# Token mix of batches 2 to 7: the last products of two chunks in the array's row halves, and beta1's term added to x by GpSimd

## The chip, the cores and the metric

The kernel runs on one core of one Trainium2 chip. The metric is the device time of one execution in microseconds (us), as a median of several. All of the work is written out by hand: every instruction stands in one engine's queue in the order in which the program emits it, and the engines wait for one another by semaphores. The engines are TensorE (PE; its weight loads are PEld), VectorE (DVE), ScalarE (ACT), GpSimd (POOL) and SyncE (SP), whose only task here is to issue transfers.

## What is computed

Attention over pooled keys and values, and then a token-mixing and a channel-mixing layer:

```python
B, H, S, D = 8, 8, 576, 64        # d_model = 512
k_p, v_p = mean of k, v over groups of 8 tokens          # 72 each
x = softmax(q @ k_p.T / 8) @ v_p, heads side by side     # (8, 576, 512)
a1 = alpha1 * x + beta1
tok = einsum('ts,bsd->btd', w_tok, a1)
u = x + lam * tok
a2 = alpha2 * u + beta2
out = u + lam * (relu(a2 @ w_ch1) @ w_ch2)               # w_ch1 512x2048
```

A batch has 576 tokens: 4 chunks of 128 and a rest of 64. In the mix, `lam * tok` is a product of `w_tok` with `lam * alpha1 * x`, plus a term of beta1 alone: the sum of the row t of `w_tok`, times `lam * beta1`.

## The kernel before, in words

**Chunks and blocks.** Batches go in pairs. A pair has nine chunks of 128 tokens: four of the even batch, four of the odd one, and a mixed one made of the 64 last tokens of both (c = 4). The 36 chunks are cut into NBLK = 9 blocks of four. The loop at the end of the program goes over the blocks: block n does the channel mix (`mlp_A`, `mlp_B`) of its 512 tokens, and beside it the attention and the token mix of batch b = n + 1, which later blocks need. Blocks 7 and 8 have no attention beside them.

**Order.** In each block everything is put in a list `todo` of pairs (due time, function), and the list is sorted by due time and called in that order. This is the order in which all engines get their instructions. `mlp_A(n, j)` is due at j, for j from 0 to 15, with four products of 128x512 into a PSUM bank; the 16 parts of `mlp_B` are due at 16 to 31, four products each. `attention(b)` (a function in the program) gives the due times of the rest: `sum_k` and `att_K` (keys), `att_V` (values), `att_S4` (the scores of four heads, in row halves of the array) with its exponentials `exp(k)` on ScalarE, `att_AV` (a head's output, into `x`), `att_X` and `rest_X` (`xs`, which is `x * lam * alpha1` in bf16), `mix_T` (a chunk's token mix), `mix_uT` (the transpose of its result, for `mlp_A`), `cast_rem` and `att_Frem` (the last 64 tokens of q and k of the next batch: cast on POOL, and their q transposed by a transfer).

**The token mix.** `mix_T(b, c)` adds up five products into one bank `ps_tok`. Four take 128 tokens each. The fifth takes the 64 last tokens. For an even batch these lie in rows 0 to 63 of `xs[:, 4]`, row 64 holds `lam * beta1`, and row 64 of `wtT[:, 4]` holds the row sums of `w_tok`: 65 rows give the product and beta1's term together. For an odd batch the tokens lie in rows 64 to 127 with the beta1 row at row 0 (`wtT[:, 5]`), and all 128 rows are used. In the mixed chunk the two batches' halves of the output go to columns 0 to 63 and 64 to 127 of the array, side by side, ten products in all. VectorE then adds `x` (`u_sb`, L613) and multiplies by alpha2 (`u_bf`, L616); SP issues the transpose of `u_bf` (L625, into `u_fm`).

**Queues.** SP's queue carries, in due order, the outputs (L695, L699), the u_fm transposes (L625), the rem_qT transpose (L415), the transposes of the next batch's q (qT, L391), and the loads of v (L160), of k (L93) and of the remainders (L148). An issue in it that waits holds up all behind it. POOL's queue carries the loads of q (L79), `sum_k` (L183, L185), some of `att_X` (L577, L570) and `cast_rem` (L168, L171).

**Buffers.** `x_tm` has one buffer for a pair of batches, six sections of 128 tokens; an even batch uses sections 1 to 5, an odd one 0 to 4. `u_sb` has twelve buffers, q_bf four. All banks of PSUM but two come from one pool of six (`gp`).

Of the kernel before, what the change touches and what calls it, by code (L numbers as in the profile page):

```python
# [7 lines left out]
FP = mybir.dt.float32  # L8
F16 = mybir.dt.float16
BF = mybir.dt.bfloat16  # L10
AF = mybir.ActivationFunctionType
ALU = mybir.AluOpType
AX = mybir.AxisListType

P = 128
SPG = 72
DM = 512
# [6 lines left out]
def kernel(  # L24
# [18 lines left out]
    nc = tc.nc  # L43
    ctx.enter_context(tc.manual_schedule())
    B, H, S, D = q.shape

    const = ctx.enter_context(tc.tile_pool(name="const", bufs=1))
# [4 lines left out]
    def gp(name):  # L52
        return psA.tile([P, 512], FP, tag="gp", name=name)
# [11 lines left out]
    st1 = {}  # L65
# [307 lines left out]
    def setup_bias(js):  # L373
        ps_bias = gp("ps_bias")
        for i, jc in enumerate(js):
            for cc in range(4):
                nc.tensor.matmul(out=ps_bias[0:P, i:i + 1], lhsT=w1_of(cc, jc),
                                 rhs=b2c_bf[:, cc:cc + 1], start=(cc == 0), stop=(cc == 3))
        nc.scalar.copy(out=bias_cols[:, js[0]:js[-1] + 1], in_=ps_bias[0:P, 0:len(js)])
# [120 lines left out]
    def att_S4(b, u):  # L500

        st = st1[b]
        qT, kp, rest = st["qT"][u], kp_pool[u], st["rem_qT"]
        lo = [psB.tile([P, DM], FP, tag="ch", bufs=2, name="ps_s") for _ in range(2)]
        hi = [gp("ps_s") for _ in range(2)]
        r = [gp("ps_r")[0:SPG, 0:128].rearrange("p (h i) -> p h i", i=64) for _ in range(2)]

        def main(i):
            for a in range(2):
                rows = slice(64 * a, 64 * a + 64)  # L510
                nc.tensor.matmul(  # L511
                    out=(hi if i > 1 else lo)[a][0:SPG, 256 * (i % 2):256 * (i % 2) + 256],
                    lhsT=kp[rows, i, :], rhs=qT[rows, 2 * i:2 * i + 2, :])

        def rests(i):
            for a in range(2):
                rows = slice(64 * a, 64 * a + 64)
                nc.tensor.matmul(  # L518
                    out=r[a][:, i // 2], lhsT=kp[rows, i + a, :],
                    rhs=rest[rows, :, 2 * u + i // 2::4].rearrange("p c i -> p i c"))  # L520

        pairs = ((lo, 0), (hi, 2)) if u else ((hi, 2), (lo, 0))
        main(pairs[0][1])
        rests(pairs[0][1])
        main(pairs[0][1] + 1)
        main(pairs[1][1])
        rests(pairs[1][1])
        main(pairs[1][1] + 1)
        ET = ET_pool[u]
        for i in range(4):  # L530
            st["ET"][4 * u + i] = ET[:, i]

        def exp(k):
            if k < 2:
                o, i = ET[:, k::2, 512:S], r[k]
            else:
                a, (pair, h) = k % 2, pairs[k // 2 - 1]
                o = ET[:, h:h + 2, 256 * a:256 * a + 256]
                i = pair[a][0:SPG, :].rearrange("p (h i) -> p h i", i=256)
            nc.scalar.activation(out=o, in_=i, func=AF.Exp, bias=0.0, scale=0.125)  # L540

        st["exp", u] = exp

    def att_AV(b, h):
        st = st1[b]
        if "x" not in st:
            st["x"] = st1[b - 1]["x"] if b % 2 else work.tile([P, 6, DM], FP, tag="x_tm", bufs=1, name="x_tm")
        hp, hh = h // 2, h % 2
        ET, vp1, x = st["ET"][h], vp1_pool[hp], st["x"]
        ps_av = gp("ps_av")  # L550
        av = ps_av[:, 0:5 * 66].rearrange("p (c x) -> p c x", x=66)
        odd = b % 2
        for c in range(4):
            m0 = 256 * (c % 2) + 128 * (c // 2)
            nc.tensor.matmul(out=av[:, odd + c, :], lhsT=ET[:, m0:m0 + 128],  # L555
                             rhs=vp1[:, hh, :])

        r0 = 512 - 64 * odd
        nc.tensor.matmul(out=av[:, 4 - 4 * odd, :], lhsT=ET[:, r0:r0 + 128], rhs=vp1[:, hh, :])  # L559
        rec = work.tile([P, 5], FP, tag="rec", bufs=2, name="rec")  # L560
        nc.vector.reciprocal(out=rec, in_=av[:, :, 64:65])  # L561
        dd = D * h
        nc.vector.tensor_tensor(out=x[:, 1 - odd:6 - odd, dd:dd + D], in0=av[:, :, 0:64],  # L563
                                in1=rec.unsqueeze(2).to_broadcast((P, 5, D)), op=ALU.mult)

    def rest_X(b, h0, h1, eng=nc.vector):

        x, xs = st1[b]["x"], xs_pool[b % 2]
        cols, p0 = slice(D * h0, D * h1), 64 * (b % 2)
        eng.tensor_tensor(out=xs[p0:p0 + 64, 4, cols], in0=x[p0:p0 + 64, 5 - 5 * (b % 2), cols],  # L570
                          in1=lamal_bc[p0:p0 + 64, cols], op=ALU.mult)

    def att_X(b, h0, h1, eng=nc.vector, rest=True):

        x, xs = st1[b]["x"], xs_pool[b % 2]
        cols = slice(D * h0, D * h1)
        eng.tensor_tensor(  # L577
            out=xs[:, 0:4, cols], in0=x[:, 1:5, cols],
            in1=lamal_bc[:, cols].unsqueeze(1).to_broadcast((P, 4, D * (h1 - h0))), op=ALU.mult)
        if rest:  # L580
            rest_X(b, h0, h1, eng)


    st2 = {}
# [11 lines left out]
    def keep_warm(count):  # L596

        ps = psB.tile([P, DM], FP, tag="ch", bufs=2, name="ps_warm")
        for _ in range(count):
            nc.tensor.matmul(out=ps, lhsT=warm[:, 0:P], rhs=warm)  # L600

    def mix_T(b, c, eng=nc.vector):
        key, s = chunk_of(b, c)
        ps_tok = gp("ps_tok")
        parts = ((b % 2, 0, P),) if c < 4 else ((0, 0, 64), (1, 64, P))
        for sc in range(5):
            for i, p0, p1 in parts:
                kk, at = (P, sc) if sc < 4 else (P, 5) if i else (65, 4)
                nc.tensor.matmul(out=ps_tok[p0:p1], lhsT=wtT[0:kk, at, P * c:P * c + p1 - p0],  # L609
                                 rhs=xs_pool[i][0:kk, sc, :], start=(sc == 0), stop=(sc == 4))  # L610
        for i, p0, p1 in parts:
            x = st1[b - b % 2 + i if c == 4 else b]["x"]
            nc.vector.tensor_tensor(out=s["u"][p0:p1, :],  # L613
                                    in0=x[p0:p1, 1 + c if c < 4 else 5 - 5 * i, :],
                                    in1=ps_tok[p0:p1, 0:DM], op=ALU.add)
        eng.tensor_tensor(out=s["u_bf"], in0=s["u"], in1=al2_bc, op=ALU.mult)  # L616
# [172 lines left out]
    def attention(b):  # L789
# [11 lines left out]
        if b < B - 1:  # L801
            at = 28.5 if first else 10.0
            todo.append((at, lambda: att_F(b + 1, 0)))
            todo.append((at + 0.1, lambda: att_F(b + 1, 2)))
            todo.append((25.6 if first else 24.5, lambda: cast_rem(b + 1, nc.gpsimd)))
            todo.append((27.5, lambda: att_Frem(b + 1)))
        for u in range(2):
            todo.append((3.6 + 0.1 * u if first else -0.9 + 1.2 * u,
                         lambda u=u: sum_k(b, u, nc.gpsimd)))
# [2 lines left out]
        for u in range(2):  # L812
            at = (9.0 if first else 6.3, 13.6)[u]
            todo.append((at, lambda u=u: att_S4(b, u)))
            for k, dt in enumerate((0.1, 0.1, 0.1, 0.7, 1.7, 1.75) if u else (0.1, 0.1, 0.1, 1.1, 2.1, 3.1)):
                todo.append((at + dt, lambda u=u, k=k: st1[b]["exp", u](k)))
            early = (5.7, 6.2, 4.2, 4.7) if first else (5.7, 6.2, 2.9, 3.4)
            for i, dt in enumerate((2.9, 3.4, 4.6, 5.1) if u else early):
                h = 4 * u + i
                todo.append((at + dt, lambda h=h: att_AV(b, h)))  # L820
                if i % 2:
                    eng = nc.gpsimd if h == 5 or first and h < 5 else nc.vector
                    todo.append((at + dt + 0.1, lambda h=h, eng=eng: att_X(b, h - 1, h + 1, eng)))
        if first:
            for i, u in enumerate((0, 2, 1)):
                todo.append((10.6 + 0.1 * i, lambda u=u: sum_v(b, u)))
            for u in range(2):
                todo.append((12.3 + 1.0 * u, lambda u=u: first_V(b, u)))
        for hp in range(0 if first else 4):
            todo.append((0.2 + 2.0 * hp, lambda hp=hp: att_V(b, hp)))  # L830
        for c in range(5):
            at = 21.0 + 1.3 * c
            if c < 4 or b % 2:
                todo.append((at, lambda c=c: mix_T(b, c)))
                key = (b, c) if c < 4 else (b - 1, 4)
                todo.append((at + 1.8, lambda key=key: mix_uT(key)))
        return todo

    for n in range(NBLK):
# [11 lines left out]
        if n == 0:  # L851
            todo.append((6.2, lambda: setup_rowsum(4)))
            todo.append((8.3, setup_wtok_odd))
            for g in range(2, 4):
                todo.append((4 * g - 0.8, lambda g=g: setup_bias(range(4 * g, 4 * g + 4))))
        if n == NBLK - 1:
            for g in range(4):
                todo.append((2.0 + 3.0 * g, lambda g=g: scale_w2(g)))
# [48 lines left out]
```

## Time and profile before

| what | us |
|---|---|
| median of 3 runs (345.4 to 347.31) | 345.45 |
| the profiled execution | 346.01 |
| its span | 344.3 |
| block 0 with the end of the start-up, 27.7 to 67.8 | 40.1 |
| block 1, mix of batch 2 | 35.4 |
| block 2, mix of batch 3 and the mixed chunk | 36.8 |
| block 3, mix of batch 4 | 35.4 |
| block 7, channel mix alone | 27.6 |

The page comes from one profiled execution, which is 0.56 us above the median. Blocks are read off the chain of work in order of time, at the first `ps_h` of each. A row of the timeline gives a start, a length, an engine and what it does; a row of the list of waits gives who waited for whom, the sum, how often, and the longest. The clock granted to TensorE is 1.0 through the whole span.

### The profile page before, as it was taken

To read this page: it belongs to the slowest core of one execution; us is meant where nothing else is said; L and a number is where in the kernel's file an instruction comes from. 1 tells how busy PE (TensorE), PEld (TensorE's weight loads), DVE (VectorE), ACT (ScalarE), POOL (GpSimd) and SP (SyncE) were. 2 spreads that over 40 slices of the span, in tenths; PEclk is the share of its full clock that TensorE was granted. 3 is DMA by queue.
4 is the path that set the end of the run, shared out by engine and by line. 5 is a ranking of instruction groups with operands and counts; after the bars stand their busy time and mean duration, and the time that the engine had idled before them with its cause. 6 is when DMAs were issued, how large, how long until landed. Compare 5 with 4: busy or idle time off the path is not lost.

```text
span 344.3 us, 5882 instructions
## 1 busy us (share of the span) xinstructions
PE 336.2 (98%) x2204; PEld 177.4 (52%) x2204; DVE 221.2 (64%) x477; ACT 146.8 (43%) x277; POOL 94.8 (28%) x110
## 2 busy tenths in 40 slices
PE   7999999999999999999999999899999999999995
PEld 2768754455445544455455544454455445545544
DVE  6772478975868586866776688558675882037511
ACT  3767950089007910484038402680089006604700
POOL 8869367310162014501260217002600100000000
PEclk9999999999999999999999999999999999999999
DMA  8999979959589816794789257971900132011012
GB/s 119 198 211 275 275 142 276 172 138 161 147 233 178 148 30 184 154 208 48 208 171 179 48 170 153 190 110 61 252 32 1 47 76 76 2 61 62 2 52 70
DMA packets 66030, 45.76 MB, mean 133 GB/s; under 512 B 34345, under 2 KB 56237, under 8 KB 66002
## 3 DMA queue, kind: packets, MB, share of 16 engines
q1 hardware_dynamic: 51716, 32.73, 40.3%
q0 software_dynamic: 13824, 12.40, 22.2%
q8 instruction: 17, 0.28, 0.3%
q10 hardware_dynamic: 462, 0.27, 0.3%
q14 instruction: 11, 0.09, 0.1%
HBM read 38.30 MB, written 9.44 MB: 139 GB/s over the span
## 4 chain that ended last, share of the span: by engine, by line
PE 86%; DMA 7%; DVE 4%; issue 1%; POOL 0%; ACT 0%; SPq 0%; DVEq 0%; POOLq 0%
PE ps_h L651 35%; PE ps_ch L686 29%; PE ps_tok L609 10%; DMA u_fm<-u_bf 3%; PE ps_av L555 2%; PE ps_s L511 2%; DMA rem_qT<-rem_q 2%; DMA q_bf<-in_q_dram 2%; DVE u_sb L613 1%; PE ps_ch L675 1%; DVE u_bf L616 1%; PE ps_kp L439 1%; PE ps_r L518 1%; PE ps_sc L491 1%; DVE ps_ch L692 1%
## 5 line engine op out<-in xcount | busy, mean ns | idle before, releaser
L657 ACT ACTIVATE Hj<-ps_h,bias_cols 128x512 bf16<-128x512 f32 x144 | 98.2, 688 | 165.5 <-PE ps_h L651 163.9
L651 PE MATMUL ps_h<-u_fm,w 128*128 128x512 bf16 (+2 forms) x608 | 133.6, 368 | 0.7 <-DMA u_fm<-u_bf 0.3
L686 PE MATMUL ps_ch<-w,Hj 128*128 128x512 bf16 x560 | 130.9, 379 | 0.0
L651 PEld LDWEIGHTS <-w 128*128 128x128 bf16 x608 | 65.5, 114 | 52.0 <-issue 4.1
L686 PEld LDWEIGHTS <-Hj 128*128 128x128 bf16 x560 | 52.9, 98 | 61.7 <-issue 1.6
L609 PE MATMUL ps_tok<-xs,wtT 128*128 128x512 bf16 (+3 forms) x200 | 44.9, 380 | 0.1
L577 POOL TENSOR_TENSOR xs<-x_tm,lamal_bc 128x512 bf16<-128x512 f32 x12 | 15.2, 1269 | 107.9 <-DVE x_tm L563 107.8
L692 DVE TENSOR_TENSOR ps_ch<-lam_bc,ps_ch 128x512 f32<-128x512 f32 x32 | 22.1, 692 | 32.4 <-PE ps_ch L686 32.2
L613 DVE TENSOR_TENSOR u_sb<-x_tm,ps_tok 128x512 f32<-128x512 f32 (+1 forms) x40 | 27.3, 683 | 11.2 <-PE ps_tok L609 11.2
L561 DVE RECIPROCAL rec<-ps_av 128x5 f32<-128x5 f32 x64 | 12.3, 192 | 34.4 <-PE ps_av L559 34.1
L563 DVE TENSOR_TENSOR x_tm<-ps_av,rec 128x320 f32<-128x320 f32 x64 | 31.5, 491 | 2.7
L693 DVE TENSOR_TENSOR u_sb<-u_sb,ps_ch 128x512 f32<-128x512 f32 x35 | 24.0, 687 | 13.6 <-PE ps_ch L686 12.5
L540 ACT ACTIVATE ET<-ps_s 72x512 f16<-72x512 f32 x56 | 32.3, 592 | 0.0
L616 DVE TENSOR_TENSOR u_bf<-u_sb,al_bc 128x512 bf16<-128x512 f32 x34 | 26.2, 770 | 3.2 <-DMA u_fm<-u_bf 2.1
L609 PEld LDWEIGHTS <-wtT 128*128 128x128 bf16 (+3 forms) x200 | 17.3, 100 | 21.2 <-issue 1.7
L479 DVE TENSOR_TENSOR v_u<-v_u 72x512 f32<-72x512 f32 (+1 forms) x48 | 26.4, 550 | 0.8
L183 POOL TENSOR_TENSOR k_raw<-k_raw 128x512 f32<-128x512 f32 x14 | 18.2, 1303 | 10.0 <-DMA k_raw<-in_k_dram 10.0
L185 POOL TENSOR_TENSOR k_bf<-k_raw 128x512 bf16<-128x512 f32 x14 | 18.8, 1343 | 1.1
L555 PEld LDWEIGHTS <-ET 72*128 72x128 f16 x256 | 13.9, 97 | 9.3 <-DVE vp L472 0.6
L79 POOL DMA_DIRECT2D q_bf<-in_q_dram x16 | 12.6, 792 | 14.2 <-DVE v_u L158 13.4
L555 PE MATMUL ps_av<-vp,ET 72*128 72x66 f16 x256 | 15.6, 193 | 0.0
L577 DVE TENSOR_TENSOR xs<-x_tm,lamal_bc 128x512 bf16<-128x512 f32 x20 | 14.8, 738 | 0.7
(130 smaller groups left out, 215.8 us busy)
## 6 DMA issues: line engine op xcount, KB each, us to landing
out_dram<-u_sb SPq DMA_DIRECT2D x32, 256.0 KB
k_raw<-in_k_dram SPq DMA_DIRECT2D x12, 512.0 KB
v_u<-in_v_dram SPq DMA_DIRECT2D x12, 512.0 KB
q_bf<-in_q_dram POOLq DMA_DIRECT2D x16, 256.0 KB, 6.2
w<-in_moe_w_ch_dram POOLq DMA_DIRECT2D x6, 512.0 KB, 12.7
w<-in_moe_w_ch_dram POOLq DMA_DIRECT2D x1, 1024.0 KB, 14.5
k_raw<-in_k_dram POOLq DMA_DIRECT2D x2, 512.0 KB, 16.8
v_main<-in_v_dram POOLq DMA_DIRECT2D x1, 1024.0 KB, 11.6
```

Of the source, the lines that this page charges most:

```text
L479: nc.vector.tensor_tensor(out=t[:, :, 0:n], in0=t[:, :, 0:n], in1=t[:, :, n:2 * n], op=ALU.add)
L540: nc.scalar.activation(out=o, in_=i, func=AF.Exp, bias=0.0, scale=0.125)
L555: nc.tensor.matmul(out=av[:, odd + c, :], lhsT=ET[:, m0:m0 + 128], rhs=vp1[:, hh, :])
L563: nc.vector.tensor_tensor(out=x[:, 1 - odd:6 - odd, dd:dd + D], in0=av[:, :, 0:64], in1=rec.unsqueeze(2).to_broadcast((P, 5, D)), op=ALU.mult)
L577: eng.tensor_tensor(out=xs[:, 0:4, cols], in0=x[:, 1:5, cols], in1=lamal_bc[:, cols].unsqueeze(1).to_broadcast((P, 4, D * (h1 - h0))), op= ...
L609: nc.tensor.matmul(out=ps_tok[p0:p1], lhsT=wtT[0:kk, at, P * c:P * c + p1 - p0], rhs=xs_pool[i][0:kk, sc, :], start=(sc == 0), stop=(sc == 4))
L613: nc.vector.tensor_tensor(out=s["u"][p0:p1, :], in0=x[p0:p1, 1 + c if c < 4 else 5 - 5 * i, :], in1=ps_tok[p0:p1, 0:DM], op=ALU.add)
L616: eng.tensor_tensor(out=s["u_bf"], in0=s["u"], in1=al2_bc, op=ALU.mult)
L651: nc.tensor.matmul(out=ps_h[:, t0:t1 + one], lhsT=w1_of(cc, j), rhs=rhs, start=(cc == 0), stop=(cc == 3))
L657: nc.scalar.activation(out=t, in_=ps_h, func=AF.Relu, bias=bias_cols[:, j:j + 1], scale=1.0)
L686: nc.tensor.matmul(out=ps, lhsT=Hj[n, j][:, 128 * m:128 * m + 128], rhs=w2[j // 4][:, j % 4, :], start=(j == 0), stop=(j == NJ - 1))
L692: nc.vector.tensor_tensor(out=ps, in0=lam_bc, in1=ps, op=ALU.mult)
```

## The change

The 64 last tokens of batches 2 to 7 are now written to both halves of the rows: `exp` writes their scores twice, `att_AV` gives all 128 rows of the fifth section, and `rest_X` writes 128 rows of `xs`. In `mix_T`, chunks go in pairs (0 and 1, 2 and 3). With the even chunk go its four full products, and then both chunks' fifth products, one from rows 0 to 63 (`wtT[0:64, 4]`), one from rows 64 to 127 (`wtT[64:128, 5]`), into two banks; with the odd chunk go its four full products alone. In the mixed chunk the fifth products take 64 rows each.

The term of beta1 leaves the product. `load_be1` loads beta1 on SP at 28.2 of block 0, into a buffer of `u_sb`. At 1.6 and 2.0 of block 1, POOL multiplies it by lam, TensorE turns the row sums into columns by six products (`setup_rcol`), ScalarE copies them, and POOL makes `tokc`, six sections of 128x512. In each of blocks 1 to 6, POOL adds `tokc` to `x` in place: heads 0 to 3 in one instruction at 12.7, after their `xs` are made; heads 4 to 7 in five instructions from 18.9.

Three due times move: the mix of batch 1 from 21.0 + 1.3c to 20.8 + 1.2c (with its transposes 1.8 later each), and `att_Frem` from 27.5 to 26.22 in block 0 and 26.72 in the others.

```diff
         def exp(k):
             if k < 2:
                 o, i = ET[:, k::2, 512:S], r[k]
+                if b > 1:
+                    o = ET[:, k::2, 512:S + 64].rearrange("p h (r i) -> p h r i", i=64)
+                    i = i.unsqueeze(2).to_broadcast((SPG, 2, 2, 64))
...
-        r0 = 512 - 64 * odd
+        r0 = 512 if b > 1 else 512 - 64 * odd
...
-        eng.tensor_tensor(out=xs[p0:p0 + 64, 4, cols], in0=x[p0:p0 + 64, 5 - 5 * (b % 2), cols],
-                          in1=lamal_bc[p0:p0 + 64, cols], op=ALU.mult)
+        rows = slice(p0, p0 + 64) if b < 2 else slice(0, P)
+        eng.tensor_tensor(out=xs[rows, 4, cols], in0=x[rows, 5 - 5 * (b % 2), cols],
+                          in1=lamal_bc[rows, cols], op=ALU.mult)
...
+    def load_be1():
+        late["be1"] = work.tile([P, DM], FP, tag="u_sb", bufs=12, name="be1_bc")
+        late["tokc"] = const.tile([P, 6, DM], BF, tag="wt_bf", name="tokc")
+        nc.sync.dma_start(out=late["be1"], in_=moe_beta1.unsqueeze(0).to_broadcast((P, DM)))
+
+    def setup_rcol():
+        nc.gpsimd.tensor_tensor(out=late["be1"], in0=late["be1"], in1=lam_bc, op=ALU.mult)
+        ps = gp("ps_rc")
+        for i, t0 in enumerate((448, 0, 128, 256, 384, 512)):
+            nc.tensor.matmul(out=ps[:, i:i + 1], lhsT=wtT[64:65, 4, t0:t0 + P],
+                             rhs=ones_bf[64:65, 0:1])
+        nc.scalar.copy(out=rcol, in_=ps[:, 0:6])
+
+    def setup_tokc(i):
+        nc.gpsimd.tensor_scalar(out=late["tokc"][:, i], in0=late["be1"], scalar1=rcol[:, i:i + 1],
+                                scalar2=None, op0=ALU.mult)
+
+    def add_tokc(b, h0, h1, n0, n1):
+
+        x, cols = st1[b]["x"], slice(D * h0, D * h1)
+        nc.gpsimd.tensor_tensor(out=x[:, n0:n1, cols], in0=x[:, n0:n1, cols],
+                                in1=late["tokc"][:, n0:n1, cols], op=ALU.add)
...
     def mix_T(b, c, eng=nc.vector):
         key, s = chunk_of(b, c)
-        ps_tok = gp("ps_tok")
         parts = ((b % 2, 0, P),) if c < 4 else ((0, 0, 64), (1, 64, P))
-        for sc in range(5):
+        if b > 1 and c < 4:
+            if c % 2 == 0:
+                ps_mix[c], ps_mix[c + 1] = gp("ps_tok"), gp("ps_tok")
+            ps_tok, xs = ps_mix[c], xs_pool[b % 2]
+            for sc in range(4):
+                nc.tensor.matmul(out=ps_tok, lhsT=wtT[:, sc, P * c:P * c + P], rhs=xs[:, sc, :],
+                                 start=(c % 2 == 0 and sc == 0), stop=(c % 2 == 1 and sc == 3))
+            if c % 2 == 0:
+                for i in range(2):
+                    r = slice(64 * i, 64 * i + 64)
+                    nc.tensor.matmul(out=ps_mix[c + i],
+                                     lhsT=wtT[r, 4 + i, P * (c + i):P * (c + i) + P],
+                                     rhs=xs[r, 4, :], start=(i == 1), stop=(i == 0))
+        elif b > 1:
+            ps_tok = gp("ps_tok")
+            for sc in range(5):
+                for i, p0, p1 in parts:
+                    r, at = (slice(0, P), sc) if sc < 4 else (slice(p0, p1), 4 + i)
+                    nc.tensor.matmul(out=ps_tok[p0:p1], lhsT=wtT[r, at, P * c:P * c + p1 - p0],
+                                     rhs=xs_pool[i][r, sc, :], start=(sc == 0), stop=(sc == 4))
+        else:
+            ps_tok = gp("ps_tok")
+        for sc in range(0 if b > 1 else 5):
...
-            todo.append((27.5, lambda: att_Frem(b + 1)))
+            todo.append((26.72 if b > 1 else 26.22, lambda: att_Frem(b + 1)))
...
+        if not first:
+            s0 = 1 - b % 2
+            todo.append((12.7, lambda: add_tokc(b, 0, 4, s0, s0 + 5)))
+            for i, sec in enumerate((1, 2, 3, 4, 5 * s0)):
+                todo.append((18.9 + 0.01 * i, lambda sec=sec: add_tokc(b, 4, 8, sec, sec + 1)))
...
-            at = 21.0 + 1.3 * c
+            at = 20.8 + 1.2 * c if first else 21.0 + 1.3 * c
...
+            todo.append((28.2, load_be1))
...
+        if n == 1:
+            todo.append((1.6, setup_rcol))
+            for i in range(6):
+                todo.append((2.0 + 0.1 * i, lambda i=i: setup_tokc(i)))
```

More of the change, by code (lines that the diff above doesn't have):

```diff
@@ L581, in att_X @@
             rest_X(b, h0, h1, eng)
+    rcol = const.tile([P, 6], FP, tag="rcol", name="rcol")
+    late = {}
+    def load_be1():
[16 more added lines that the diff above has]
+                                in1=late["tokc"][:, n0:n1, cols], op=ALU.add)
     st2 = {}
@@ L600, in keep_warm @@
             nc.tensor.matmul(out=ps, lhsT=warm[:, 0:P], rhs=warm)
+    ps_mix = {}
     def mix_T(b, c, eng=nc.vector):
         key, s = chunk_of(b, c)
-        ps_tok = gp("ps_tok")
         parts = ((b % 2, 0, P),) if c < 4 else ((0, 0, 64), (1, 64, P))
-        for sc in range(5):
+        if b > 1 and c < 4:
[21 more added lines that the diff above has]
+        for sc in range(0 if b > 1 else 5):
             for i, p0, p1 in parts:
```

## The prediction, made before the changed kernel had run

> **What bounds the kernel now.** I read the page from the top: the busy shares, then the waits of TensorE, then the chain of work in order of time. The first says that TensorE works through the whole span, the second that it hardly ever waits; together the waits come to some 4 us, of which 2 us are after the start-up.
>
> ```profile
> PE 336.2 (98%) x2204; PEld 177.4 (52%) x2204; DVE 221.2 (64%) x477; ACT 146.8 (43%) x277; POOL 94.8 (28%) x110
> ```
> ```profile
> PE ps_r L518 <- DMA rem_qT<-rem_q: 1.5, 1, 1.5
> ...
> PE ps_h L651 <- DMA u_fm<-u_bf: 0.3, 1, 0.3
> ```
>
> So a saving counts only if it shortens TensorE's own stream or removes one of these waits, and any other engine's work counts only if it makes TensorE wait. Matmul ends are modelled, so I price the stream by starts. The chain over the mix of batch 3 (columns: start, length, what) gives them:
>
> ```profile
> 130.41 0.86 PE ps_ch L686 x4
> 131.27 1.08 PE ps_tok L609 x5
> 132.35 1.73 PE ps_ch L686 x8
> 134.08 1.25 PE ps_tok L609 x10
> ```
>
> A 512-column product costs 0.86 / 4 = 0.216 us, and a chunk of the mix five of them, 1.08. The mixed chunk of last tokens has ten, in five side-by-side pairs: 1.25, not 1.08. The extra 0.17 is the price of changing how the array is divided. The timeline shows the same at the scores, which already use row halves (64*72):
>
> ```profile
> 116.70 0.38 PE L651 MATMUL ps_h<-u_fm,w 128*128 128x512 bf16 x1
> 117.01 0.30 PE L511 MATMUL ps_s<-qT,kp 64*72 64x256 bf16 x2
> ```
> ```profile
> 117.34 0.27 PE L511 MATMUL ps_s<-qT,kp 64*72 64x256 bf16 x2
> 117.45 0.24 PE L518 MATMUL ps_r<-rem_qT,kp 64*72 64x64 bf16 x2
> 117.52 0.28 PE L511 MATMUL ps_s<-qT,kp 64*72 64x256 bf16 x2
> 117.73 0.41 PE L651 MATMUL ps_h<-u_fm,w 128*128 128x512 bf16 x1
> ```
>
> Going in, the next start comes 0.31 us after a full product instead of 0.216: +0.09. Coming out, 0.21 after a 256-column pair, which otherwise takes 0.11: +0.10.
>
> **What the Trainium skill says.** *TensorEngine Tiling (Array Packing)*, Key Properties: changing the tiling mode drains TensorE. The trace agrees, 0.09 and 0.10 us above. *TensorE: Matmul & The Clock Gate*, Part 3: products in different row groups run concurrently, starting some 4 ns apart. It agrees: the two scores from 117.01 end together within 0.30. *SBUF — State Buffer*, Who interferes with whom: a VectorE instruction with two SBUF inputs contends with a GpSimd one that reads SBUF. It agrees: u_bf (L616) takes 0.69, but 1.68 at 208.94, beside k_raw on POOL. *GPSIMD Engine Reference*, Engine selection: one-input operations run at about line rate, two-input ones about twice as slow. It agrees: a CAST of 128x256 takes 0.40 on POOL, a TENSOR_TENSOR of that shape 0.73.
>
> **The change part by part.**
>
> 1. *Pairs of chunks, c below 4, batches 2 to 7.* Two chunks cost 10 x 0.216 = 2.16. After: 8 full products (1.73), one pair (0.216), two mode changes (0.19): 2.13. That is 0.03 less per pair of chunks, 12 pairs: **-0.3**. The trace has no 64*128 pair. Bounds: no drain at all, 12 x 0.216 = -2.6; the halves not side by side, 12 x (2 x 0.216 + 0.19 - 0.432) = +2.3. I take the drain, as the 64*72 and the 128*64 products both pay it.
>
> 2. *The mixed chunk of batches 3, 5, 7.* It already runs side by side. Its last pair becomes 64*64 among 128*64: one mode change more, 3 x 0.09 = **+0.3** (0 to 0.6).
>
> 3. *setup_rcol,* once in block 1: six one-column products. The bias products (16 in 0.51 us) say 0.03 each, plus in and out 0.19: **+0.4** (0.2 to 0.8). ScalarE's copy and the bank it takes have a free neighbour.
>
> 4. *Block 0's mix at 20.8 + 1.2c.* The order of TensorE's instructions puts chunk 0 and the mixed chunk one part of mlp_B (0.86) earlier. Chunk 0 already has to wait:
>
> ```profile
> 51.84 1.34 DVE xs L577
> 53.18 0.05 issue
> 53.23 1.27 PE ps_tok L609 x5
> ```
>
> Its products can't start before xs is there at 53.18, so TensorE now waits 0.86 longer here. At 67.84 it waited for u_sb (0.2 in the list of waits, 0.35 by starts), which itself hangs on the u_fm transfer landing at 65.56 behind loads; that wait disappears in the delay. Net **+0.5** (0 if the transfers let everything follow; +0.9 if u_sb slides too).
>
> 5. *att_Frem earlier.* This is the 1.5 us wait. The chain and SP's queue show why:
>
> ```profile
> 212.10 0.38 SPq L695 DMA_DIRECT2D out_dram<-u_sb  x1
> 212.57 1.21 SPq L415 DMA_TRANSPOSE rem_qT<-rem_q  x1
> ```
> ```profile
> 212.57 7.37 DMA rem_qT<-rem_q
> 219.99 0.26 PE ps_r L518 x2
> ```
>
> The transpose stood behind an output that waited for VectorE until 212.1; its inputs on POOL were done by 204.3. Put before it, it issues at about 209.6, into DMA engines that are nearly idle from 211 to 213 (share 0.05). It lands well before 218.4. On SP it passes only that output; the four other moves (blocks 1, 2, 3, 5) remove nothing, as no one waited. **-1.5** (0 to -1.7). Late next there is nothing: qT landed before, and kp waits on TensorE itself.
>
> 6. *ScalarE:* the scores of the last tokens go out twice, 128 more columns. 72x128 takes 0.27 and 72x512 0.59, so 0.11 each, 0.2 per group of four heads. The exponentials are ready 0.36 us before TensorE takes the first of them (77.29 against 77.65 in block 1). **0**, with 0.15 left; with that gone, 0.1 per group, 1 us in all. The fifth product of att_AV and the 128-row rest_X have the same columns as before: 0.
>
> 7. *POOL adds.* 128x1280 at 0.73 per 256 columns is at most 3.6, by the slope between 256 and 512 columns 2.9; five of 128x256, 0.73 each, 3.6. Some 6.6 us per batch. The first goes between the xs of heads 0 to 3 and of 4 and 5, where POOL was idle for 17 us in block 4. The five start when xs of heads 6 and 7 is done (197.4) and end near 201; the first u_sb needs section 1 at 198.7, which is done at 198.2; cast_rem stands behind them on POOL and waits for rem_raw until 202.1 anyway. Meanwhile VectorE's u_bf can be held, up to 1.0 each by the row at 208.94, for two chunks; VectorE is idle for 1.3 us before 207.5, and SP takes the transposes only from 203.07. **0**; if that cover fails, up to 1 us in each of blocks 1 and 2, whose last transposes are needed at once.
>
> 8. *be1 and tokc, block 0 to 1.* The load (256 KB) is issued on SP after the mixed chunk's transpose, about 70, ahead of two qT transposes (+0.6 there, no one waits). I put its landing at 73, from the 2 us that an output of that size took in SP's queue then. POOL then does one product (1.27) and six one-input products of 512 columns, 0.8 each from twice the CAST: ready at 79. Behind them on POOL stand the q_bf loads of batch 3, which went out at 76.57. See the second rival.
>
> Everything else (SP's order, the weights, blocks 7 and 8) is as before. Sum: -0.3 + 0.3 + 0.4 + 0.5 - 1.5 = **-0.6 us**. The profiled execution took 346.01 (span 344.3, and 1.7 around it), 0.56 over the median 345.45; -0.6 on its own time is 345.4, on the median **344.8**.
>
> **The rivals.** *No drain:* the pairs of row halves enter and leave for nothing. Parts 1 and 2 give -2.6 + 0: 344.8 - 2.6 = 342.2. For it: the weights are loaded ahead elsewhere, without a pause. Against: the rows at 117.01 and 117.73. Chance 0.10.
>
> *q_bf late (the slower side):* in block 1 the q_bf loads stand behind tokc. SP's qT transposes wait for them, and out, the remainder loads, k_raw and the u_fm transposes of batch 2 stand behind those, needed by block 2 at 103.2:
>
> ```profile
> 83.63 3.15 SPq L391 DMA_TRANSPOSE qT<-q_bf  x2
> 86.88 1.15 SPq L160 DMA_DIRECT2D v_u<-in_v_dram  x2
> 91.17 0.38 SPq L695 DMA_DIRECT2D out_dram<-u_sb  x1
> ```
>
> SP has 3.1 us free before 91.17, another 0.9 comes from the delay of parts 3 and 4, and the third u_fm, about 0.8 us early, gives the last: q_bf may go out up to 4.8 us late, at 81.4. With 0.8 per product it goes out at 79; with 1.27 (as two inputs) at 81.9 (+0.5). It decides from 1.2 us per product on; at 2 us each, 86.3 and **349.7**. For it: the operation with a column of scalars isn't in the trace. Against: the CAST. Chance 0.13.
>
> *Not side by side:* the halves queue up, part 1 is +2.3: 347.4. Against: the scores. Chance 0.05.
>
> *The wait stays:* rem_qT lands late all the same, or another takes its 1.5 us: 346.3. For it: SP and the DMA engines are at their fullest there. Chance 0.15.
>
> **How the numbers follow.** The likeliest case (0.57) is 344.8, from 343.8 to 346 by the bounds of parts 2 to 6. With *the wait stays* and part of *no drain* and *not side by side*, 342.4 to 347.5 leaves out 2 in 10. One per cent is 3.45 us, about what a measurement of this kernel can tell from no change: below 342.0 lies half of *no drain* with the wait removed in full, and what I don't see, 0.12; above 348.9 most of *q_bf late* and waits of VectorE on POOL that recur in every block, 0.14; within, 0.74.
>
> **What would show it.** Right: the pair of 64*128 products starts 0.31 after a full one and the next full one 0.31 later; ps_tok in the chain falls by about 0.03 per two chunks; no wait for rem_qT; the wait before the first ps_tok of block 0 grows to about 1 us. Wrong: a pair without the extra 0.19; waits of ps_h for u_fm at the start of block 2; u_sb waiting for POOL's x_tm; a tokc product above 1.2 us.

## The result and the profile after

The changed kernel takes **350.88 us** (median of 4 runs, 349.21 to 351.69), the kernel before 345.42 in the same comparison (345.34 to 347.31): a ratio of 1.0131, 95% interval 1.0087 to 1.0176. The forecast was 344.8, with 342.4 to 347.5 as its range. The profiled execution took 350.25, its span is 348.5, 4.2 us more than that of before.

The 4.2 us are best found block by block. The table gives the time from the first `ps_h` of a block to that of the next, read off TensorE's rows in the two profiled executions; block 0 is counted from its first `ps_h` product of 128x512, before which the changed kernel is 0.13 ahead. (The table of the time before took its blocks from the pieces of the chain, which gives 35.4, 36.8 and 35.4 for blocks 1 to 3.)

| block | before | after | difference |
|---|---|---|---|
| 0 | 31.24 | 32.00 | +0.76 |
| 1 | 35.20 | 39.76 | **+4.56** |
| 2 | 36.96 | 36.99 | +0.03 |
| 3 | 35.20 | 35.78 | +0.58 |
| 4 | 36.50 | 36.61 | +0.11 |
| 5 | 36.90 | 35.19 | **-1.71** |
| 6 | 36.50 | 36.61 | +0.11 |
| 7, 8 | 59.20 | 59.13 | -0.07 |

One block carries the loss. Blocks 2 to 6, which run the same new code, are 0.9 shorter together, by block 5. The busy shares after say that TensorE's own work did not grow, while that of POOL grew by half, from 94.8 to 141.8:

```profile
PE 336.2 (96%) x2173; PEld 175.3 (50%) x2210; DVE 228.2 (65%) x477; ACT 148.4 (43%) x278; POOL 141.8 (41%) x153
```

The list of TensorE's waits after (who waited for whom: sum, how often, longest). The wait for rem_qT, 1.5 us before, is gone; two waits of the token mix for VectorE's xs are new, 1.9 and 0.5. The 0.9 is that of block 0, which was 0.05 before.

```profile
PE ps_tok L648 <- DVE xs L574: 1.9, 1, 1.9
...
PE ps_tok L663 <- DVE xs L581: 0.9, 1, 0.9
...
PE ps_tok L643 <- DVE xs L581: 0.5, 1, 0.5
...
PE ps_h L705 <- DMA u_fm<-u_bf: 0.2, 1, 0.2
```

Both new waits are in block 1. POOL's timeline there (start, length, what, and in brackets the idle time before it and what ended it) shows where they come from:

```profile
73.95 1.74 POOL L597 TENSOR_TENSOR be_bc<-be_bc,lam_bc 128x512 f32<-128x512 f32 x1 [10.29 <-DMA be_bc<-in_moe_beta_dram]
75.79 9.99 POOL L605 TENSOR_SCALAR tokc<-be_bc,rcol 128x512 bf16<-128x512 f32 x6
85.73 1.59 POOL L79 DMA_DIRECT2D q_bf<-in_q_dram  x2
87.33 2.64 POOL L611 TENSOR_TENSOR x_tm<-x_tm,tokc 128x1280 f32<-128x1280 f32 x1
89.90 1.28 POOL L581 TENSOR_TENSOR xs<-x_tm,lamal_bc 128x512 bf16<-128x512 f32 x1
91.13 0.92 POOL L574 TENSOR_TENSOR xs<-x_tm,lamal_bc 128x128 bf16<-128x128 f32 x1
92.02 2.53 POOL L611 TENSOR_TENSOR x_tm<-x_tm,tokc 128x256 f32<-128x256 f32 x4
94.85 0.67 POOL L611 TENSOR_TENSOR x_tm<-x_tm,tokc 128x256 f32<-128x256 f32 x1 [0.30 <-DVE xs L574]
```

From 73.95 to 94.55 POOL is never free, where before it was idle for 13.35 us ahead of the q_bf loads and for 9.26 ahead of its xs. The six products of tokc take 9.99 us, 1.67 each, and everything behind them is pushed into the moment when the mix needs its inputs. On VectorE's timeline, the same moment:

```profile
90.08 1.66 DVE L581 TENSOR_TENSOR xs<-x_tm,lamal_bc 128x512 bf16<-128x512 f32 x1
91.67 3.04 DVE L574 TENSOR_TENSOR xs<-x_tm,lamal_bc 128x128 bf16<-128x128 f32 x1
94.63 0.68 DVE L746 TENSOR_TENSOR ps_ch<-lam_bc,ps_ch 128x512 f32<-128x512 f32 x1
```

Before, the same two took 0.71 and 0.28 in block 1, with the second on half of the rows:

```profile
88.92 0.71 DVE L577 TENSOR_TENSOR xs<-x_tm,lamal_bc 128x512 bf16<-128x512 f32 x1
89.55 0.28 DVE L570 TENSOR_TENSOR xs<-x_tm,lamal_bc 64x128 bf16<-64x128 f32 x1
```

After, the second, now 128x128, starts at 91.67 and ends at 94.71, 0.16 after the last of POOL's four additions in a row: it lasts through all four, and POOL's fifth addition waits for it. (That it is the four that hold it is shown by two runs below, in which it takes 0.28 and 0.54.) TensorE's timeline shows the price:

```profile
91.89 1.02 PE L643 MATMUL ps_tok<-xs,wtT 128*128 128x512 bf16 x4 [0.48 <-DVE xs L581]
94.76 0.61 PE L648 MATMUL ps_tok<-xs,wtT 64*128 64x512 bf16 x2 [1.85 <-DVE xs L574]
95.31 1.89 PE L740 MATMUL ps_ch<-w,Hj 128*128 128x512 bf16 x4
```

The products from 95.31 to 97.84 started 0.40 to 0.43 us apart, not 0.216: after the waits TensorE ran at half its clock for a while. A table by windows (window, length, then busy time and instructions of PE, PEld, DVE, ACT, POOL; then PEclk, DMA share and GB/s) has it as 0.53 from 95.3 to 98.1:

```profile
91.00:95.30 4.30, 1.97 (x8) 0.43 (x6) 4.30 (x3) 0.00 (x0) 4.00 (x7) 0.91 1.06 124
95.30:98.10 2.80, 2.80 (x10) 1.01 (x9) 1.99 (x4) 0.00 (x0) 0.22 (x1) 0.53 1.06 224
98.10:108.00 9.90, 9.85 (x46) 4.32 (x46) 6.63 (x10) 0.00 (x0) 5.41 (x6) 1.00 0.95 236
```

By starts, block 1's 4.56 are: 0.64 and 1.92 at the two waits, over the steps of 0.216 and 0.312 that these products take without one; 1.50 at half clock; 0.17 in a short pause at 77.1; and 0.33 for the one-column products. The part at half clock is not in every execution: in two of the four (351.69 and 349.21 us) the mean granted clock is 1.0. The 0.2 for u_fm in the list is at the start of block 3, where before has 0.3.

### The profile page after: what moved, and what is told of

It reads as the page before. It is cut to its first block, busy times and chain, and to the rows that moved or that the text cites. A ratio compares the mean times of both kernels' runs of the same rounds, so it can differ in the third digit from the quotient of the medians.

```text
span 348.5 us, 5917 instructions
## 1 busy us (share of the span) xinstructions
PE 336.2 (96%) x2173; PEld 175.3 (50%) x2210; DVE 228.2 (65%) x477; ACT 148.4 (43%) x278; POOL 141.8 (41%) x153
## 4 chain that ended last, share of the span: by engine, by line
PE 87%; DVE 5%; DMA 4%; issue 2%; POOL 0%; ACT 0%; SPq 0%; DVEq 0%; POOLq 0%
PE ps_h L705 35%; PE ps_ch L740 31%; PE ps_tok L643 6%; PE ps_av L558 2%; DMA u_fm<-u_bf 2%; PE ps_s L511 2%; DMA q_bf<-in_q_dram 2%; PE ps_tok L648 1%; PE ps_tok L656 1%; DVE ps_ch L746 1%; PE ps_ch L729 1%; PE ps_tok L663 1%; DVE xs L574 1%; PE ps_kp L439 1%; DVE u_sb L747 1%
## 5 line engine op out<-in xcount | busy, mean ns | idle before, releaser
L740 PE MATMUL ps_ch<-w,Hj 128*128 128x512 bf16 x543 | 129.5, 381 | 0.9 <-issue 0.5
L740 PEld LDWEIGHTS <-Hj 128*128 128x128 bf16 x560 | 52.0, 98 | 61.4 <-issue 4.6
L611 POOL TENSOR_TENSOR x_tm<-x_tm,tokc 128x256 f32<-128x256 f32 (+1 forms) x36 | 35.3, 1007 | 71.2 <-DVE xs L574 67.6
L670 DVE TENSOR_TENSOR u_bf<-u_sb,al_bc 128x512 bf16<-128x512 f32 x34 | 28.4, 837 | 3.3 <-DMA u_fm<-u_bf 2.2
L479 DVE TENSOR_TENSOR v_u<-v_u 72x512 f32<-72x512 f32 (+1 forms) x48 | 27.7, 577 | 0.8
L643 PE MATMUL ps_tok<-xs,wtT 128*128 128x512 bf16 x96 | 25.1, 385 | 0.8 <-DVE xs L581 0.5
L581 POOL TENSOR_TENSOR xs<-x_tm,lamal_bc 128x512 bf16<-128x512 f32 x12 | 15.2, 1271 | 17.1 <-DVE x_tm L566 17.0
L185 POOL TENSOR_TENSOR k_bf<-k_raw 128x512 bf16<-128x512 f32 x14 | 18.9, 1352 | 1.1
L581 DVE TENSOR_TENSOR xs<-x_tm,lamal_bc 128x512 bf16<-128x512 f32 x20 | 15.5, 775 | 0.7
L643 PEld LDWEIGHTS <-wtT 128*128 128x128 bf16 x96 | 9.5, 100 | 12.7 <-issue 2.1
```

Source lines behind the costliest of these rows:

```text
L479: nc.vector.tensor_tensor(out=t[:, :, 0:n], in0=t[:, :, 0:n], in1=t[:, :, n:2 * n], op=ALU.add)
L581: eng.tensor_tensor(out=xs[:, 0:4, cols], in0=x[:, 1:5, cols], in1=lamal_bc[:, cols].unsqueeze(1).to_broadcast((P, 4, D * (h1 - h0))), op= ...
L611: nc.gpsimd.tensor_tensor(out=x[:, n0:n1, cols], in0=x[:, n0:n1, cols], in1=late["tokc"][:, n0:n1, cols], op=ALU.add)
L643: nc.tensor.matmul(out=ps_tok, lhsT=wtT[:, sc, P * c:P * c + P], rhs=xs[:, sc, :], start=(c % 2 == 0 and sc == 0), stop=(c % 2 == 1 and sc ...
L740: nc.tensor.matmul(out=ps, lhsT=Hj[n, j][:, 128 * m:128 * m + 128], rhs=w2[j // 4][:, j % 4, :], start=(j == 0), stop=(j == NJ - 1))
```

## The experiments

**Theory A:** the late tokc makes POOL's additions of batch 2 late, these hold VectorE's xs, and TensorE waits for xs. **Theory B** is the rival of the prediction: tokc makes the q_bf loads late, SP's queue stands behind them, and the u_fm that block 2 needs lands late. **Theory C:** the new mix costs block 1 its time by itself. The start-up before block 0 took 36.3 to 40.3 us in the profiled executions, whatever the kernel, so block lengths are compared, and the ratios are set beside them.

### Additions of batch 2 left out

Left out is beta1's term in batch 2; tokc is made as before.

```diff
-        if not first:
+        if b > 2:
             s0 = 1 - b % 2
             todo.append((12.7, lambda: add_tokc(b, 0, 4, s0, s0 + 5)))
```

> The changed kernel without the additions of tokc to x for batch 2 alone; what it leaves out is beta1's term in batch 2. tokc itself is still made by POOL in block 1, 10 us of it, and the q_bf loads still stand behind it. Theory A (the late additions hold VectorE's xs of heads 6 and 7[...], and the first mix of block 1 waits for xs): block 1 falls from 39.8 us to about 36, the list of TensorE's waits loses xs L574 (1.9), the clock stays at 1.0, the median is about 346. Theory B (the late q_bf loads hold SP's queue, and with it what block 1 and 2 need): nothing changes, block 1 stays at 39.8 and the median at 350.5.

Ratio 1.0152 (1.0063 to 1.0241). The waits for xs are gone, and VectorE's two xs take 0.71 and 0.28:

```profile
93.46 0.71 DVE L581 TENSOR_TENSOR xs<-x_tm,lamal_bc 128x512 bf16<-128x512 f32 x1
94.09 0.28 DVE L574 TENSOR_TENSOR xs<-x_tm,lamal_bc 128x128 bf16<-128x128 f32 x1
```

But block 1 falls only to 37.88, since its list of waits has a new first line, at the start of block 2:

```profile
PE ps_h L705 <- DMA u_fm<-u_bf: 2.2, 1, 2.2
```

It has B's cause: on SP the two transposes of q that need the late q_bf go out 20.63 us after the start of block 1 (15.79 before), and the last u_fm 35.75 (33.03 before). So A is at work in the changed kernel, and B stands right behind it: with A out of the way, the late transposes decide. Neither expectation named both. In the changed kernel B doesn't show, because TensorE was 4 us late itself.

### q_bf put ahead of tokc

```diff
-                todo.append((2.0 + 0.1 * i, lambda i=i: setup_tokc(i)))
+                todo.append((6.7 + 0.01 * i, lambda i=i: setup_tokc(i)))
```

> The changed kernel with tokc due at 6.7 instead of 2.0 in block 1, which puts the q_bf loads of batch 3 ahead of the six products on POOL. The loads go out at about 79 instead of 86, tokc ends at about 90 instead of 86, and the additions of batch 2 come later. Theory A: more of the mix's inputs wait for POOL (the xs of heads 4 and 5 stands behind the additions as well), block 1 grows from 39.8 to 42 or more, the median to 352 or more. Theory B: the wait goes, block 1 falls to about 36, the median to about 346.

Ratio 1.0124 (1.0039 to 1.021); block 1 is 39.72. The q_bf loads go out at 77.90, the two transposes of q 16.95 us after the start of the block, no u_fm is late, and the loss is the same, now as one wait of 2.3 us for POOL's own xs and again a stretch at half clock. Timeline of POOL:

```profile
77.90 1.55 POOL L79 DMA_DIRECT2D q_bf<-in_q_dram  x2 [3.39 <-DVE v_u L158]
79.47 9.61 POOL L605 TENSOR_SCALAR tokc<-be_bc,rcol 128x512 bf16<-128x512 f32 x6
89.17 2.61 POOL L611 TENSOR_TENSOR x_tm<-x_tm,tokc 128x1280 f32<-128x1280 f32 x1
91.74 1.71 POOL L581 TENSOR_TENSOR xs<-x_tm,lamal_bc 128x512 bf16<-128x512 f32 x1
```

B alone, then, explains nothing of the changed kernel's time: without it the loss stays. The 42 us that A expected did not come either: POOL's large addition starts 1.9 us later in the block than in the changed kernel (20.76 us after its start against 18.86), but the small additions no longer run beside VectorE's small xs, and the pair has no wait of its own.

### The late additions of batch 2 on VectorE

```diff
-    def add_tokc(b, h0, h1, n0, n1):
+    def add_tokc(b, h0, h1, n0, n1, eng=nc.gpsimd):
...
-        nc.gpsimd.tensor_tensor(out=x[:, n0:n1, cols], in0=x[:, n0:n1, cols],
+        eng.tensor_tensor(out=x[:, n0:n1, cols], in0=x[:, n0:n1, cols],
...
-                todo.append((18.9 + 0.01 * i, lambda sec=sec: add_tokc(b, 4, 8, sec, sec + 1)))
+                eng = nc.vector if b == 2 else nc.gpsimd
+                todo.append((18.9 + 0.01 * i,
+                             lambda sec=sec, eng=eng: add_tokc(b, 4, 8, sec, sec + 1, eng)))
```

> The changed kernel with batch 2's five late additions on VectorE instead of POOL; tokc is as late as in the changed kernel, and all is computed. Theory A1 (POOL's four additions in a row hold VectorE's xs of 128x128): that xs takes 0.3 to 1 us, not 3.04, the wait of the pair for it (1.9) goes, and with it the stretch at half clock; the pair then starts at once after chunk 0's products, and block 1 falls from 39.8 to 36.3, or to 38.2 if the u_fm of block 2 is late by up to 2 us as without the first addition. Theory A2 (POOL's queue is late as such, whoever makes the additions): the pair still waits 1.5 us or more and block 1 stays above 38.5.

("Without the first addition" in this text is the run without batch 2's additions, all six.) POOL is as late as in the changed kernel: its large addition starts at 88.24, 18.6 us after the start of block 1 (18.9 there). VectorE:

```profile
91.06 1.59 DVE L581 TENSOR_TENSOR xs<-x_tm,lamal_bc 128x512 bf16<-128x512 f32 x1
92.57 0.54 DVE L574 TENSOR_TENSOR xs<-x_tm,lamal_bc 128x128 bf16<-128x128 f32 x1
93.03 1.75 DVE L611 TENSOR_TENSOR x_tm<-x_tm,tokc 128x256 f32<-128x256 f32 x5
```

The xs takes 0.54, not 3.04, and the pair's wait is gone: A1, VectorE held by POOL's four additions, is shown. Of the xs waits only the 0.4 for L581 is left, beside POOL's xs. The time is no better, 1.0131 (1.0074 to 1.0188): B takes 2.6 us at the start of block 2 and, behind it, half clock from 109.8 to 113.2. Block 1 is 38.88, 0.7 over what was expected: u_fm costs 2.77 by starts where up to 2 were expected.

### One product of six taken out of the way

Section 0 of tokc, which batch 2 doesn't read, is made after batch 2's additions.

```diff
-                todo.append((2.0 + 0.1 * i, lambda i=i: setup_tokc(i)))
+                todo.append((2.0 + 0.1 * i if i else 19.5, lambda i=i: setup_tokc(i)))
```

> The changed kernel with the product for section 0 of tokc, which batch 2 does not read, made by POOL after batch 2's additions: POOL has five products of 1.6 us ahead of q_bf and the additions in block 1, not six. All is computed. Theory A (late additions hold VectorE's xs and with it TensorE): the additions come 1.6 us earlier, the waits of ps_tok for xs, 3.3 us together, fall to about 1 to 2 and the half clock behind them goes or shortens; block 1 falls from 39.8 to 36.5 to 38.2 us. Theory C (the new scheme costs block 1 its time by itself, whenever tokc is ready): 39.8 again.

Ratio 1.0035 (1.0002 to 1.0068); block 1 is **36.74**, within what A expected, and the waits for xs are gone altogether, where A had left 1 to 2 us of them. One product less is not the whole difference in this profile: POOL's large addition starts 2.65 us earlier in the block (16.21 us after its start), 1.4 of it from the five products, 0.5 because beta1 times lam took 1.27 and not 1.74, and 0.8 because that began earlier. From these 2.65 us the block gains 3.0: no wait for xs, no half clock, and B falls from the 2.2 that it is without A to 1.0 in the list of waits:

```profile
PE ps_h L705 <- DMA u_fm<-u_bf: 1.0, 1, 1.0
PE ps_tok L663 <- DVE xs L581: 0.9, 1, 0.9
```

### Tokc where POOL is idle; the new mix from batch 4

```diff
-        if not first:
+        if b > 3:
...
-            todo.append((28.2, load_be1))
...
         if n == 1:
+            todo.append((28.2, load_be1))
+        if n == 2:
             todo.append((1.6, setup_rcol))
             for i in range(6):
-                todo.append((2.0 + 0.1 * i, lambda i=i: setup_tokc(i)))
+                todo.append((5.5 + 0.1 * i, lambda i=i: setup_tokc(i)))
```

The other tests for b in the new code become b > 3 too.

> The changed kernel with the new mix, the doubled rows and the additions from batch 4 on; batches 2 and 3 as before; beta1 is loaded at 28.2 of block 1, and tokc is made in block 2 from 5.5 on, where nothing behind it on POOL is due. All is computed. Theory A/B (it is the six products ahead of q_bf and of batch 2's additions): block 1 is 35.2 again, no wait of ps_tok for xs in it, no wait of ps_h for u_fm at block 2's start; the span is that of before, 344.3, less 1.5 to 1.7 for rem_qT, plus 0.6 to 0.8 for block 0, plus 0.2 to 0.4 for the six one-column products: 343.4 to 344. Theory C: blocks 3 to 5 lose what block 1 loses, at least 2 us: 346 or more.

Ratio 1.0014 (0.9987 to 1.0042). Blocks 1 to 6 are 35.63, 36.96, 35.18, 36.60, 35.19 and 36.61. In block 2 the products cost nothing, with nothing due behind them; they take 1.56 each:

```profile
112.59 1.26 POOL L597 TENSOR_TENSOR be_bc<-be_bc,lam_bc 128x512 f32<-128x512 f32 x1 [3.75 <-DMA be_bc<-in_moe_beta_dram]
113.96 9.35 POOL L605 TENSOR_SCALAR tokc<-be_bc,rcol 128x512 bf16<-128x512 f32 x6
```

Block 1's +0.43 is a wait for u_fm at its end. Its cause is open: the load of beta1 is issued after its transposes, and one of the two runs with the earlier att_Frem alone, which has nothing of the new mix, loses 0.34 at the same place. From the first product of block 0 on, the kernel is 0.65 us shorter than before. C falls: blocks 3 to 6 run the new mix with its additions at the price of before, to 0.1 (block 5 has lost the wait for rem_qT besides).

### The same, with batch 1's mix back, and that move alone

```diff
-            at = 20.8 + 1.2 * c if first else 21.0 + 1.3 * c
+            at = 21.0 + 1.3 * c
```

> As the last one, with batch 1's mix back at 21.0 + 1.3c. If the earlier mix of batch 1 costs block 0 the 0.6 to 0.8 us that it shows, the end of block 0 is 67.8 again and the span falls by as much against the last one: 342.8 to 343.3. Against before with the earlier att_Frem alone (span 341.7) what is left, 1 to 1.6 us, is then the price of the new mix itself: one-column products, mixed chunks, less the pairs.

> The kernel before with batch 1's mix at 20.8 + 1.2c and nothing else. Predicted +0.5 (0 to 0.9); the changed kernel shows block 0 ending 0.6 to 0.8 later. If that is the due times alone, block 0 ends at 68.4 to 68.6 here, the wait before the first ps_tok at 53 is 0.9 to 1.1 us, and blocks 1 to 8 are as before, with the 1.5 us wait for rem_qT; the span is 344.8 to 345.1. If it needs the load of beta1 and the other edits, block 0 ends at 67.8.

Ratios 1.0025 (0.9984 to 1.0066) and 1.0038 (1.0009 to 1.0067). Alone, the move makes block 0 31.76, +0.52 over before, with the wait of 0.9 before its first ps_tok: the due times are the cause. Seven of the nine kernels with the move have 31.73 to 31.76. Without it the block varies with how late the first product of block 1 comes: 30.97 and 31.05 where it is 0.08 and 0.16 late (att_Frem alone, twice), 31.24 with 0.35 (the kernel before), 31.38 with 0.50 in the first of these two runs. Less that lateness all four are 30.9, so the move costs 0.87, and +0.52 is what remains when before's own 0.35 is gone. The first of the two runs was expected to be shorter in all than the version before it, and is not: u_fm was late at the start of blocks 1, 2 and 3, 1.3 us together.

### Tokc on VectorE, and on ScalarE

```diff
-        nc.gpsimd.tensor_scalar(out=late["tokc"][:, i], in0=late["be1"], scalar1=rcol[:, i:i + 1],
+        nc.vector.tensor_scalar(out=late["tokc"][:, i], in0=late["be1"], scalar1=rcol[:, i:i + 1],
```

due at 6.6 + 0.01i; and

```diff
+        nc.scalar.activation(out=late["tokc"][:, i], in_=late["be1"], func=AF.Copy, bias=0.0,
+                             scale=rcol[:, i:i + 1])
```

due at 7.1 + i, in place of POOL's product.

> The changed kernel with the six products of tokc made by VectorE at 6.6 of block 1, in the idle time before its first outputs of the attention; all is computed. POOL then has only be1 by lam (1.7 us) ahead of the q_bf loads. Theory A and theory B both expect block 1 at 36 to 36.5 and a median of about 345.3, the prediction's sum with the wait away; the cost of the six on VectorE is 0.3 to 0.6 us each. If neither POOL's 10 us nor what stands behind them is the cause, the median stays at 350.

> The changed kernel with the six products of tokc on ScalarE, one in each part of mlp_A from 7.1 on; POOL does beta1 times lam alone. All is computed. If the late tokc on POOL is the whole of the loss, block 1 has no wait of ps_tok for xs and none of ps_h for u_fm at block 2's start: 35.6 to 35.9 us (35.2, the 0.47 of the six one-column products, and up to 0.2 for ScalarE). The sum against before is then +0.5 (block 0), +0.5 (block 1), +0.4 at most (start of block 4), +0.1 and +0.1 (mixed chunks), -1.7 (rem_qT) and up to -0.3 (u_fm wait at 140): -0.5 to 0, as was predicted for the change itself; ratio 0.997 to 1.001. If the additions cost every block something, blocks 2 to 6 are longer than in the changed kernel.

On VectorE a product takes 0.48, the ratio is 1.0053 (1.0023 to 1.0084), block 1 is 36.82, a little over what was expected: the waits for xs and the half clock are gone, but the six delay VectorE's x, and TensorE waits 0.5 for it before scores, and 0.3 by starts for u_fm at the start of block 2.

On ScalarE the expectation failed: 1.0079 (1.0046 to 1.0112), block 1 is 37.88. In block 1 and at the start of block 2 no xs and no u_fm is late, but ScalarE itself had no room. Its timeline in that stretch is without a gap:

```profile
84.31 0.73 ACT L605 ACTIVATE tokc<-be_bc,rcol 128x512 bf16<-128x512 f32 x1
84.92 0.69 ACT L711 ACTIVATE Hj<-ps_h,bias_cols 128x512 bf16<-128x512 f32 x1
85.49 0.73 ACT L605 ACTIVATE tokc<-be_bc,rcol 128x512 bf16<-128x512 f32 x1
86.11 0.69 ACT L711 ACTIVATE Hj<-ps_h,bias_cols 128x512 bf16<-128x512 f32 x1
86.68 0.74 ACT L605 ACTIVATE tokc<-be_bc,rcol 128x512 bf16<-128x512 f32 x1
87.29 0.70 ACT L711 ACTIVATE Hj<-ps_h,bias_cols 128x512 bf16<-128x512 f32 x1
```

and TensorE waits for its Hj and its exponentials; block 1 is 2.3 longer than 35.2 and the 0.33 for the one-column products. An engine that is 43% busy over the span can be full in the one stretch that matters.

> As the last one, with batch 1's mix back at 21.0 + 1.3c. Block 0 is then 0.4 to 0.8 shorter, unless the load of beta1, which stands on SP ahead of nothing that block 1 needs at once, delays its first ps_h; the sum against before is -0.4 to -1.3. It should still be 0.3 to 1 us slower than before with the earlier att_Frem alone, by the one-column products (0.47) and the mixed chunks (0.3), less the pairs (0.1).

With batch 1's mix back besides, the ratio is 1.0094 (1.0061 to 1.0128): block 0 was 32.36, not shorter, with a wait of 0.8 for u_fm at its end and one of 0.3 for VectorE's vp in it. The load of beta1 is issued after that transpose, and isn't the cause.

### att_Frem alone

```diff
-            todo.append((27.5, lambda: att_Frem(b + 1)))
+            todo.append((26.72 if b > 1 else 26.22, lambda: att_Frem(b + 1)))
```

> The kernel before with the two due times of att_Frem moved, 26.22 in block 0 and 26.72 after, and nothing else. By part 5 of the prediction the wait of ps_r for rem_qT (1.5 us by the list, 1.7 by starts) goes and no other comes: block 5 falls from 36.9 to 35.2 and the median from 345.4 to 343.7. The rival (the wait stays or moves) says 345.4.

> The kernel before with the earlier att_Frem alone, again, beside the last two: the wait for rem_qT gone (1.7 us by starts), nothing added. Blocks 1 to 8 were 274.3 us where before has 276.5; expected again within 0.3, and a ratio of 0.993 to 0.997. Of the four it should be the fastest.

345.39 us twice, against 347.39 and 346.72 for before in those comparisons: 0.9969 (0.9937 to 1.0000) and 0.9964 (0.9942 to 0.9986). Block 5 is 35.20 both times, and blocks 1 to 8 take 274.30 and 274.65 against 276.46 before. SP's timeline: the transpose goes out at 208.76 and no longer at 212.57, and the output behind it waits for VectorE by itself.

```profile
204.75 3.92 SPq L625 DMA_TRANSPOSE u_fm<-u_bf  x3
208.76 1.20 SPq L415 DMA_TRANSPOSE rem_qT<-rem_q  x1
211.27 0.38 SPq L695 DMA_DIRECT2D out_dram<-u_sb  x1
```

It is the only version here that beats the kernel before: the due times of one step, out of the whole change.

## Why the prediction was wrong

**The step that failed is part 8**, "six one-input products of 512 columns, 0.8 each from twice the CAST: ready at 79". They took 1.67 each in block 1 and 1.56 undisturbed. A CAST of 256 columns says little about a product with a column of scalars, and the line rate that the prediction cites for one-input operations does not hold for it: the same product took 0.48 on VectorE. Be1 landed at 73.9 (73 was said) and its product took 1.74 (1.27), so POOL was free at 85.8. Of the signs of being wrong that the prediction named, a product above 1.2 us is the one that came.

That alone would have made the second rival decide, which does so "from 1.2 us per product on". By that rival's sum the q_bf loads, out at 85.73, are 4.3 us beyond its slack (81.4), and the time is 349.1. Its chain exists, but where A was out of the way it cost 2.2 and 2.6 us by the list of waits, and in the changed kernel it costs nothing: that 349.1, or its 349.7 at 2 us, came near the result is chance. **The second failure is part 7's cover.** It costed the additions at nothing for the times at which they run when tokc has long been there, and named u_bf as what VectorE could lose. Tokc came 7 us late, so the large addition of batch 2 started 18.86 us after the start of its block, that of batch 3 15.43, and the four small ones ran beside VectorE's xs, which nothing covers: TensorE takes it at once. Waits for xs and the half clock behind them made 4.06 of block 1's 4.56. The right question was what stands on POOL behind tokc, not only q_bf but the additions and the xs, and beside which VectorE instructions they then run.

The rest of the sum held:

- *Part 1* (-0.3): the mode changes are real, and *no drain* is out. The timeline of batch 3's mix after:

```profile
130.48 1.03 PE L643 MATMUL ps_tok<-xs,wtT 128*128 128x512 bf16 x4
131.44 0.39 PE L648 MATMUL ps_tok<-xs,wtT 64*128 64x512 bf16 x2
131.76 1.04 PE L740 MATMUL ps_ch<-w,Hj 128*128 128x512 bf16 x4
```

 By starts, the pair comes 0.312 after the last full product and the next full product 0.322 after it: 0.634 where two fifths and the step on take 0.648, 0.014 less per pair of chunks, not 0.03. The 12 pairs save 0.2.
- *Part 2* (+0.3): blocks 4 and 6 are 0.11 longer with two pairs in each, so the mixed chunk costs 0.14; three make 0.4.
- *Part 3* (+0.4): 0.33 by starts, way in and out included, in block 1 and again in block 2 of the version from batch 4. That block is 0.47 longer (36.96 against the 36.49 of att_Frem alone), but 0.10 of it is a late first product of block 3, so the 0.47 that later expectations took for these products is too much.
- *Part 4* (+0.5): +0.52 alone, with the longer wait at the first ps_tok and the 0.35 gone, both as predicted; about +0.8 against a block 0 without that 0.35.
- *Part 5* (-1.5): -1.71.
- *Part 6* (0): no wait for ScalarE in the changed kernel. How little room it has in block 1 is seen with tokc on it.
- *Part 7* from block 2 on: the large addition takes 2.61 and the small ones 0.67 each (2.9 to 3.6 and 0.73 were said), and no wait in TensorE's list is put down to them.

With ScalarE making tokc, blocks 1 to 8 take 277.57 us against 276.46; take off the 2.3 of ScalarE and add block 0's 0.5, and it is -0.7, beside the predicted -0.6. This is an estimate, not a run: no version with tokc in time for batch 2 without a new wait was found.

**Open:** the 0.6 in block 3 after. The first ps_h of block 4 starts 0.4 to 0.7 late in six of the eight kernels with the new mix from batch 2, 0.1 late and in time in the other two. The last u_fm transpose before it goes out 32.17 us after the start of block 3 where block 4 is 0.4 late (the run with one product of six moved) and 32.21 where it is in time (tokc on ScalarE), so the time of issue is not the cause; the lists of waits name no single one, and it stays open, as do the waits for u_fm at other blocks that are left open above.

## What to carry to other kernels

Price a set-up step by the same operation with the same kinds of operands, or keep the whole range: then ask what stands behind it in its engine's queue, and beside which short instruction of another engine the displaced work will run. Put such a step where nothing due stands behind it; ten microseconds on POOL cost 4 us in block 1 and none in block 2. When a late step feeds two chains, taking away the wait that shows uncovers the other: the two have to be treated at their common root.

## What the runs showed of the hardware

- *One VectorE instruction held by several POOL ones.* The Trainium skill, *SBUF — State Buffer*, Who interferes with whom, calls the port pair that VectorE shares with GpSimd an exclusive lock. Here a product that takes 0.28 us alone took 3.04 and ended only after four additions in a row had: VectorE didn't get in between them.
- *The same product on three engines* (128x512, a column of scalars, float32 to bf16): 1.56 us on POOL, 0.48 on VectorE, 0.73 on ScalarE.
- *Half clock after short waits.* The Trainium skill, *TensorE: Matmul & The Clock Gate*, Part 1, gives half clock after an idle window of about 3.4 us. Here the clock fell in a block three times, each time for 3.41 us (from 94.49 in the changed kernel; from 94.91 with q_bf ahead of tokc; from 109.81 with the late additions on VectorE), and each time a whole number of such stretches after it first goes to full in the start-up (25, 25 and 28 after 9.16, 9.57 and 14.24). In the 3.41 us just before, TensorE had been idle for 2.06, 2.01 and 2.11 us, so the stretch need not be idle throughout. The wait of 2.2 us in the run without batch 2's additions is cut by the same grid: 1.9 us of idle time fall between 108.03 and 111.44, 0.3 before, and the clock stayed. So a wait of some 2 us can cost 1.5 more or nothing, by where it falls on the grid. Whether there is a sharp limit between 1.9 and 2.0 us was not tested. In a start-up the clock once fell after a stretch with 0.5 us of idle time and many small products (18.62, tokc on ScalarE), so idle time by the profile is not all that decides.
